# Masks subtracted one slot later, and the Exp of two duos put ahead of the exit, in a top-32 attention followed by a two-layer MLP

## The chip, the cores and the metric

The kernel runs on one core of a Trainium2 chip. Its engines work at the same time, each on its own queue in order: TensorE (PE, matmuls and their weight loads), VectorE (DVE), ScalarE (ACT), GpSimd (POOL) and SyncE (SP, which here only issues DMAs). The metric is the device time of one execution in microseconds (us). The time before is 880.53 us, the median of 3 runs (880.13 to 882.18).

## The reference

Eight batches of eight heads, 576 tokens, head size 64. Each row of scores keeps its 32 largest entries, and the result goes through an MLP whose activation has a learned slope for negative values:

```
scores = (1/8) * q @ k^T                       # 576 x 576 per head
kth    = 32nd largest of each row
scores = where(scores >= kth, scores, -1e9)
attn   = softmax(scores) @ v
x      = heads side by side                    # 4608 x 512
h      = x @ w_in                              # 4608 x 2048
out    = (max(h,0) + alpha * min(h,0)) @ w_out # 4608 x 512
```

All inputs and the output are float32.

## The kernel before

**The unit of work is a duo:** two tiles of 128 query rows, one of each head of a pair of heads ("n"), or the last 64 rows of each head of two pairs ("m", mixed). There are 144 duos (ND), 18 per batch, of which two are mixed. The main loop has one slot per duo, n = 0 to ND + 6, and in slot n each stage works on another duo. Every engine's instructions are kept in the order in which the program writes them, except where the planner moves one ahead of a neighbour that is not ready by its own estimate; the small VectorE instructions of a slot are moved now and then.

**The stages of duo m** (for Exp and norm, m is the even one of two duos m, m+1 that share a tile):

| stage | engine | lines | slot |
|---|---|---|---|
| st_qk: scores to PSUM (one buffer, ps_sc) | PE | 198-218 | m-2 |
| st_exit: scores to SBUF (s_sb) | ACT | 220-225 | m-1 |
| dve_slot: the 8 largest of each of 6 groups (up, small), from these a guess p for the 32nd | DVE | 232-299 | m |
| st_count: sg = sign(p - s), and its sum cs | ACT | 301-308 | m+1 |
| st_y: y = s * sg, so that the entries just below p become y's largest | POOL | 310-315 | m+1 |
| eq, MAX8 p<-y, pk: which of p and the next 8 is the 32nd, by the count | DVE | 271-299 | m+1 |
| kt_sum: KT = 2^60 times the 32nd largest | DVE | 227-230 | m+2 |
| st_relu: r = relu(KT - 2^60 s), zero for kept entries | ACT | 317-322 | m+2 |
| the subtraction s = s - r (masked entries fall far down) | POOL | 323 | m+2 |
| st_exp: w = exp(s/8) of two duos, then two DMA transposes w to wT | ACT, SP | 325-332 | m+4 (even) |
| st_av: xo = wT @ [v, 1] | PE | 334-353 | m+6 |
| norm_a, norm_b: x = xo / row sum, of two duos | DVE | 359-378 | m+7 (odd) |
| st_xT: DMA transpose of x, when a chunk of tokens is complete | SP | 387-409 | m+7 |

**The MLP** works on chunks of 128 or 256 tokens as attention completes them. mlp_ready (415) makes *units* (ph = x @ a piece of w_in, then VectorE's relu gT) and *parts* (a quarter of an output tile pz, four parts a = 0 to 3; the part with a = 3 ends the tile and puts a *store* in a list). The slope's linear share is folded into a matrix w_lin made in the first slots (scale_out, in_trans, lin). h_pe issues a unit, h_dve its relu, o_pe a part (none while a store is open), o_act the copy of a finished tile by ScalarE (o_sb), o_sp its store. `late` (624) asks for a second unit in a slot. keep_warm fills TensorE with idle matmuls ("rest").

**The order within slot n** before (614-660): loads and stores on SP; PE: st_av(n-6), a unit; ACT: st_count(n-1); POOL: st_y(n-1); ACT: st_exit(n+1); PE: perhaps a part; DVE: dve_slot; ACT and POOL: st_relu(n-2) with its subtraction; POOL: cast of v (4 in 18 slots, even ones); PE: transposes for a later pair of heads (prep), st_qk(n+2), then a part or keep_warm; in even slots ACT: st_exp(n-4); ACT: copies of the transposes; in odd slots o_act, and at the end st_xT. After the loop a second loop empties the lists.

Buffers that matter: ps_sc one; s_sb three pairs of duos; sg and r share a tag of three; y three; w two (ws); wT three; ps_h (ph, prep, rest) two.

Of the kernel before, what the change touches and what calls it, by code (L numbers as in the profile page):

```python
# [35 lines left out]
def fast_path(tc, q, k, v, moe_w_in, moe_w_out, moe_alpha, out, flag):  # L36
# [27 lines left out]
    with ExitStack() as ctx:  # L64
# [67 lines left out]
        ws = [const.tile([128, 2, 2, 640], BF16, name=f"w_{i}") for i in range(2)]  # L132
# [99 lines left out]
        def dve_slot(n, f_late):  # L232
# [7 lines left out]
            norm = on(n - 6) and n % 2  # L240
            if on(n):
                s = T["s", n]
                up = two.tile([128, 2, NG // 2, 8], FP32, name="up", tag="up")
                for i in range(2):
                    for g in range(NG):
                        o = 24 * i + 8 * (g // 2)
                        m = DVE.max(out=(lo if g % 2 else up)[:, i, g // 2, :],
                                    in_=s[:, i, GW * g:GW * g + GW])
                        if g % 2:
                            sm(m, [], [(o, o + 8)])  # L250
                        if i == 0 and g == 1:
                            kt_sum(n - 2)
                if norm:
                    norm_a(n - 6)


                bot = two.tile([128, 2, NG // 2, 8], FP32, name="bot", tag="bot")
                sm(DVE.tensor_tensor(bot, up, lo[:, :, :, ::-1], ALU.min), [(0, 48)], [f"bot{n % 2}"])
                sm(DVE.tensor_tensor(th[:, :, 0:24].rearrange("p i (g c) -> p i g c", g=NG // 2), up,
                                     lo[:, :, :, ::-1], ALU.max), [(0, 48)], [(48, 72), (80, 104)])  # L260
                if norm:
                    norm_b(n - 6)
                for i in range(2):
                    o = 48 + 32 * i
                    sm(DVE.max(out=th[:, i, 24:32], in_=bot[:, i, :, :]), [f"bot{n % 2}"], [(o + 24, o + 32)])
            else:
                kt_sum(n - 2)
                if norm:
                    norm_a(n - 6)
                    norm_b(n - 6)  # L270
# [30 lines left out]
        def st_count(n):  # L301
            s, p9 = T["s", n], T["p9", n]
            sg = two.tile([128, 2, S], BF16, name="sg", tag="sg", bufs=3)
# [6 lines left out]
        def st_y(n):  # L310
            y = [three.tile([128, S], FP32, name="y", tag="y") for _ in range(2)]
            sg = T.pop(("sg", n))
            for i in range(2):
                POOL.tensor_tensor(y[i], T["s", n][:, i, :], sg[:, i, :], ALU.mult)
            T["y", n] = y

        def st_relu(n, i):
            s = T["s", n]
            if i == 0:
                T["r", n] = two.tile([128, 2, S], BF16, name="r", tag="sg", bufs=3)  # L320
            r = T["r", n]
            ACT.activation(r[:, i, :], s[:, i, :], AF.Relu, bias=KT[:, 2 * n + i:2 * n + i + 1], scale=-BIG)
            POOL.tensor_tensor(s[:, i, :], s[:, i, :], r[:, i, :], ALU.subtract)

        def st_exp(n):

            w = ws[n // 2 % 2]
# [175 lines left out]
        for b in range(1, B):  # L503
            for i in range(KPB):
# [6 lines left out]
                for u in range(3):  # L511
                    at(s0 + ((1, 3, 3) if b < B - 1 else (0, 1, 2))[u], "prep", lambda p=p, u=u: prep_pe(p, u))
# [101 lines left out]
        for n in range(ND + 7):  # L614
# [5 lines left out]
            if on(n - 6):  # L620
                st_av(n - 6)
            if not h_pe() and not end:
                keep_warm()
            late = len(hq) > (9 if n < 118 else 4) or end

            if on(n - 1):
                st_count(n - 1)
                st_y(n - 1)
            if on(n + 1):
# [11 lines left out]
            if on(n + 2):  # L641
# [6 lines left out]
            if on(n - 3) and n % 2 == 0:  # L648
                st_exp(n - 4)
# [6 lines left out]
            if n % 2 or end:  # L656
                o_act()
            if on(n - 6) and n % 2:
                st_xT(n - 7)
                st_xT(n - 6)  # L660
# [298 lines left out]
```

## Time and profile before

| what | us |
|---|---|
| median of 3 runs | 880.53 |
| the profiled execution's own time | 879.53 |
| its span, first to last instruction | 877.6 |
| y on GpSimd, 288 times 1.281 | 362.6 busy |
| subtraction on GpSimd, 288 times 1.283 | 362.9 busy |
| sg on ScalarE, 288 times 0.771 | 220.7 busy |
| Exp on ScalarE, 72 times 2.116 | 152.4 busy |
| exit on ScalarE, 144 times 1.105 | 159.1 busy |
| gT on VectorE, 144 times 0.676 | 97.3 busy |

The mean granted TensorE clock was 0.977. In the tables of the profile an instruction is named out<-in by the program's tiles; since a helper records every operation, all have line L31, and one goes by the tiles. A wait is written "engine, tile <- who ended it". In the order of time, each line has start, length, engine, operation, and in brackets the idle time before it with what ended it. Consecutive instructions overlap a little at their ends, so what one costs its engine is the distance from start to start: 0.67 and 0.09 for a count, 1.00 for an exit, 0.67 for a relu, 2.02 for an Exp, 0.16 for a MAX8 over 96 entries.

### The profile page before, as it was taken

The numbers are of one execution on the slowest core, as the hardware profiler recorded it, in microseconds if no ns is written. First come the engines' busy times: TensorE is split into PE (matmuls) and PEld (weight loads), VectorE is DVE, ScalarE is ACT, GpSimd is POOL, SyncE is SP. The second block draws the span as 40 slices with busy tenths as digits, with TensorE's granted clock in tenths as the row PEclk, the third lists the DMA queues.
The fourth block names the chain that finished last, engine by engine and source line by source line (L and its number), as shares of the span: only waits on it lengthen the run. The fifth ranks groups of instructions, "written<-read, shape, count | busy, mean of one in ns | idle before, by whom it ended". The sixth has DMA issues, their size and how long they took to land.

```text
span 877.6 us, 18856 instructions
## 1 busy us (share of the span) xinstructions
PE 794.9 (91%) x5531; PEld 448.5 (51%) x5626; DVE 784.2 (89%) x3921; ACT 776.4 (88%) x1239; POOL 752.1 (86%) x672
## 2 busy tenths in 40 slices
PE   8767999989899999899999998899999998999894
PEld 5333455555455555455555555555555554555462
DVE  5989899998999989999999989999999988899941
ACT  6999999898989989999999989999999988788840
POOL 4998998898988989999999989989999988798830
PEclk9989999999999999999999999999999998999997
DMA  7899845544544446446446555447455542434341
GB/s 159 184 205 177 164 107 102 116 111 105 118 112 115 113 84 122 105 110 126 115 103 140 101 113 128 105 112 129 97 118 109 114 114 68 98 80 77 91 91 34
DMA packets 344464, 100.31 MB, mean 114 GB/s; under 512 B 338193, under 2 KB 338209, under 8 KB 344353
## 3 DMA queue, kind: packets, MB, share of 16 engines
q1 hardware_dynamic: 341456, 92.42, 50.0%
q0 software_dynamic: 1696, 6.30, 3.1%
q8 instruction: 46, 0.75, 0.4%
q14 instruction: 66, 0.53, 0.2%
q10 hardware_dynamic: 1200, 0.30, 0.2%
HBM read 36.71 MB, written 9.44 MB: 53 GB/s over the span
## 4 chain that ended last, share of the span: by engine, by line
DVE 35%; PE 29%; POOL 13%; ACT 11%; issue 8%; DMA 3%; SPq 0%; POOLq 0%; ACTq 0%
PE ps_sc L31 10%; DVE p L31 10%; DVE small L31 9%; POOL y L31 8%; PE pz L31 6%; DVE up L31 5%; POOL s_sb L31 5%; DVE gT L31 5%; PE ph L31 4%; PE xo L31 4%; PE rest L31 4%; ACT sg L31 4%; ACT r L31 3%; ACT s_sb L31 2%; DMA wT<-w 1%
## 5 line engine op out<-in xcount | busy, mean ns | idle before, releaser
L31 POOL TENSOR_TENSOR y<-s_sb,sg 128x576 f32<-128x576 f32 x288 | 362.6, 1281 | 88.4 <-ACT sg L31 81.6
L31 POOL TENSOR_TENSOR s_sb<-s_sb,r 128x576 f32<-128x576 f32 x288 | 362.9, 1283 | 1.2 <-ACT r L31 1.0
L31 ACT ACTIVATE sg<-s_sb,p 128x576 bf16<-128x576 f32 x288 | 220.7, 771 | 25.5 <-DVE p L31 20.5
L31 DVE MAX8 p<-y 128x8 f32<-128x576 f32 x288 | 215.6, 748 | 20.2 <-POOL y L31 19.9
L31 DVE MAX8 small<-s_sb 128x8 f32<-128x96 f32 x864 | 216.0, 250 | 0.0
L31 DVE MAX8 up<-s_sb 128x8 f32<-128x96 f32 x864 | 211.7, 245 | 3.1 <-ACT s_sb L31 3.1
L31 ACT ACTIVATE r<-s_sb,KT 128x576 bf16<-128x576 f32 x288 | 208.4, 776 | 0.1
L31 PE MATMUL ps_sc<-qkT 64*128 64x512 f32 (+2 forms) x768 | 185.2, 573 | 21.9 <-ACT s_sb L31 20.6
L31 ACT COPY s_sb<-ps_sc 128x1152 f32<-128x1152 f32 x144 | 159.1, 1105 | 2.3 <-PE ps_sc L31 2.1
L31 PE MATMUL ph<-xT,w_in_b 128*128 128x256 bf16 (+1 forms) x1408 | 152.4, 256 | 2.7 <-DMA xT<-x 2.7
L31 ACT ACTIVATE w<-s_sb 128x2304 bf16<-128x2304 f32 x72 | 152.4, 2116 | 2.0 <-POOL s_sb L31 2.0
L31 PE MATMUL pz<-w_out_b,gT 128*128 128x512 bf16 x556 | 145.0, 381 | 5.8 <-DVE gT L31 2.3
L31 PEld LDWEIGHTS <-wT 128*128 128x128 bf16 (+3 forms) x1600 | 98.7, 100 | 70.6 <-DMA wT<-w 10.8
L31 PE MATMUL xo<-v,wT 128*128 128x65 bf16 (+3 forms) x1600 | 126.8, 198 | 7.3 <-DMA wT<-w 7.2
L31 PE MATMUL rest<-idle 128*128 128x512 bf16 x434 | 121.5, 392 | 3.1 <-ACT qkT L31 1.0
L31 DVE TENSOR_SCALAR gT<-ph 128x512 bf16<-128x512 f32 x144 | 97.3, 676 | 24.8 <-PE ph L31 24.8
L31 PEld LDWEIGHTS <-w_in_b 128*128 128x128 bf16 x1408 | 109.1, 98 | 19.7 <-DMA xT<-x 3.3
L31 PEld LDWEIGHTS ps_sc<-qkT 64*128 64x128 f32 (+1 forms) x768 | 55.4, 170 | 79.9 <-ACT s_sb L31 41.3
L31 PEld LDWEIGHTS ps_sc<-kd,qkT 128*128 128x128 f32 x256 | 39.3, 193 | 101.7 <-issue 93.4
L31 PEld LDWEIGHTS <-gT 128*128 128x128 bf16 x576 | 56.3, 98 | 57.0 <-DVE gT L31 3.6
L31 PE MATMUL ps_sc<-kd,qkT 128*128 128x128 f32 x256 | 64.3, 334 | 1.5 <-DMA kd<-qkT 1.5
L31 PEld LDWEIGHTS <-idle 128*128 128x128 bf16 x468 | 45.7, 101 | 36.0 <-issue 6.0
(56 smaller groups left out, 670.1 us busy)
## 6 DMA issues: line engine op xcount, KB each, us to landing
k_st<-in_k_dram SPq DMA_DIRECT2D x64, 128.0 KB, 2.8
v_st<-in_v_dram SPq DMA_DIRECT2D x64, 128.0 KB, 2.6
out_dram<-o_sb SPq DMA_DIRECT2D x32, 256.0 KB, 2.2
q_st<-in_q_dram SPq DMA_DIRECT2D x62, 128.0 KB, 2.7
w_st<-in_moe_w_out_dram POOLq DMA_DIRECT2D x4, 1024.0 KB, 7.2
wT<-w SPq DMA_TRANSPOSE x144, 3.1
w_in_b<-in_moe_w_in_dram POOLq DMA_DIRECT2D x4, 512.0 KB, 6.4
k_st<-in_k_dram SPq DMA_DIRECT2D x32, 32.0 KB, 2.6
```

Source lines behind the costliest of these rows:

```text
L31: return self.tc.keep_in_program_order(f(*a, **kw))
```

## The change

In each pipeline the later stages move by one slot, and with them the parity of what is done in every second slot. The subtraction leaves st_relu and becomes st_sub(n-3): the first head's stands ahead of y in GpSimd's order, the second's behind it. st_exp runs in odd slots, for duos n-5 and n-4, right behind st_count and ahead of st_exit. st_av, norm and st_xT are one slot later, norm in even slots and, in VectorE's order, behind the min/max pair (norm_a) and behind the two MAX8 of bot (norm_b). o_act and the transposes for later pairs move to even slots, `late` to odd ones; in odd slots st_qk(n+2) stands behind the part or filler. sg and r have four buffers, w one. The loop has one slot more.

```diff
-        ws = [const.tile([128, 2, 2, 640], BF16, name=f"w_{i}") for i in range(2)]
+        ws = [const.tile([128, 2, 2, 640], BF16, name=f"w_{i}") for i in range(1)]
...
-            norm = on(n - 6) and n % 2
+            norm = on(n - 7) and n % 2 == 0
...
-                if norm:
-                    norm_a(n - 6)
 
 
                 bot = two.tile([128, 2, NG // 2, 8], FP32, name="bot", tag="bot")
...
                 if norm:
-                    norm_b(n - 6)
+                    norm_a(n - 7)
                 for i in range(2):
                     o = 48 + 32 * i
                     sm(DVE.max(out=th[:, i, 24:32], in_=bot[:, i, :, :]), [f"bot{n % 2}"], [(o + 24, o + 32)])
+                if norm:
+                    norm_b(n - 7)
             else:
                 kt_sum(n - 2)
                 if norm:
-                    norm_a(n - 6)
-                    norm_b(n - 6)
+                    norm_a(n - 7)
+                    norm_b(n - 7)
...
-            sg = two.tile([128, 2, S], BF16, name="sg", tag="sg", bufs=3)
+            sg = two.tile([128, 2, S], BF16, name="sg", tag="sg", bufs=4)
...
         def st_y(n):
             y = [three.tile([128, S], FP32, name="y", tag="y") for _ in range(2)]
             sg = T.pop(("sg", n))
+            if on(n - 2):
+                st_sub(n - 2, 0)
             for i in range(2):
                 POOL.tensor_tensor(y[i], T["s", n][:, i, :], sg[:, i, :], ALU.mult)
             T["y", n] = y
+            if on(n - 2):
+                st_sub(n - 2, 1)
 
         def st_relu(n, i):
             s = T["s", n]
             if i == 0:
-                T["r", n] = two.tile([128, 2, S], BF16, name="r", tag="sg", bufs=3)
+                T["r", n] = two.tile([128, 2, S], BF16, name="r", tag="sg", bufs=4)
             r = T["r", n]
             ACT.activation(r[:, i, :], s[:, i, :], AF.Relu, bias=KT[:, 2 * n + i:2 * n + i + 1], scale=-BIG)
+
+        def st_sub(n, i):
+            s, r = T["s", n], T["r", n]
             POOL.tensor_tensor(s[:, i, :], s[:, i, :], r[:, i, :], ALU.subtract)
 
         def st_exp(n):
 
-            w = ws[n // 2 % 2]
+            w = ws[0]
...
-                    at(s0 + ((1, 3, 3) if b < B - 1 else (0, 1, 2))[u], "prep", lambda p=p, u=u: prep_pe(p, u))
+                    at(s0 + ((0, 2, 2) if b < B - 1 else (0, 1, 2))[u], "prep", lambda p=p, u=u: prep_pe(p, u))
...
-        for n in range(ND + 7):
+        for n in range(ND + 8):
...
-            if on(n - 6):
-                st_av(n - 6)
+            if on(n - 7):
+                st_av(n - 7)
             if not h_pe() and not end:
                 keep_warm()
-            late = len(hq) > (9 if n < 118 else 4) or end
+            late = len(hq) > (9 if n < 118 else 4) and n % 2 == 1 or end
 
             if on(n - 1):
                 st_count(n - 1)
                 st_y(n - 1)
+            elif on(n - 3):
+                st_sub(n - 3, 0)
+                st_sub(n - 3, 1)
+            if on(n - 4) and n % 2:
+                st_exp(n - 5)
             if on(n + 1):
                 st_exit(n + 1)
...
-            if on(n + 2):
+            if on(n + 2) and n % 2 == 0:
                 st_qk(n + 2)
             if (n, "lin") in todo:
                 run(n, "lin")
             elif not (end or ready() > 2) or not o_pe():
                 if not end:
                     keep_warm()
-            if on(n - 3) and n % 2 == 0:
-                st_exp(n - 4)
+            if on(n + 2) and n % 2:
+                st_qk(n + 2)
...
-            if n % 2 or end:
+            if n % 2 == 0 or end:
                 o_act()
-            if on(n - 6) and n % 2:
+            if on(n - 7) and n % 2 == 0:
+                st_xT(n - 8)
                 st_xT(n - 7)
-                st_xT(n - 6)
```

## The prediction

> **What bounds the kernel now.** I first read the busy shares, then who waited for whom, then the order of time within two slots in the steady middle, and last the same for the places where a slot is unusually long. The busy shares come first:
>
> ```profile
> PE 794.9 (91%) x5531; PEld 448.5 (51%) x5626; DVE 784.2 (89%) x3921; ACT 776.4 (88%) x1239; POOL 752.1 (86%) x672
> ```
>
> No engine stands out. Four engines are within 5% of each other, so a slot (one duo, about 5.6 us) is set by small waits handed from one engine to the next. The view of waits shows which are large:
>
> ```profile
> POOL y L31 <- ACT sg L31: 81.6, 76, 11.2
> ACT o_sb L31 <- PE pz L31: 48.5, 13, 13.6
> DVE gT L31 <- PE ph L31: 24.8, 16, 4.1
> ACT sg L31 <- DVE p L31: 20.5, 29, 1.8
> DVE p L31 <- POOL y L31: 19.9, 33, 2.3
> DVE rz L31 <- PE xo L31: 16.4, 18, 3.9
> DVE small L31 <- ACT sg L31: 10.1, 20, 1.4
> ```
>
> The columns are total us, times, longest. GpSimd's 81.6 us in front of the sign products y looks like the prize, but GpSimd is not what the others wait for: VectorE waits for y only 19.9 us in all. In the stretch from 150 to 750 us VectorE waits 35 us in total (14.2 for y, 7.9 for ph, 7.3 for the counts, 5.8 for xo), so 6% of it is all that a perfect reordering could return there. The order of time shows how the 81.6 us arise (start, length, engine, operation):
>
> ```profile
> 425.52 2.11 ACT L31 ACTIVATE w<-s_sb 128x2304 bf16<-128x2304 f32 x1
> 427.53 0.76 ACT L31 ACTIVATE sg<-s_sb,p 128x576 bf16<-128x576 f32 x1
> 428.46 2.52 POOL L31 TENSOR_TENSOR y<-s_sb,sg 128x576 f32<-128x576 f32 x2 [0.88 <-ACT sg L31]
> 433.45 2.52 POOL L31 TENSOR_TENSOR y<-s_sb,sg 128x576 f32<-128x576 f32 x2
> ```
>
> ScalarE's slot with an Exp (even) lasts two counts 1.52, exit 1.00, two relus 1.34 and Exp 2.02, together 5.88 us from one sg to the next, while VectorE's slot without a norm lasts 5.14 (pk to pk). So the counts after an Exp start about 0.75 us late; y shows it as 0.88. VectorE hides most of that, because it needs y only some 2.9 us into its slot. The third kind of place is one slot in which ScalarE stands at a store:
>
> ```profile
> 511.61 0.59 ACT L31 COPY o_sb<-pz 128x512 f32<-128x512 f32 x1 [2.82 <-PE pz L31]
> 513.03 2.51 POOL L31 TENSOR_TENSOR y<-s_sb,sg 128x576 f32<-128x576 f32 x2 [2.91 <-ACT sg L31]
> 514.35 0.76 DVE L31 MAX8 p<-y 128x8 f32<-128x576 f32 x1 [2.33 <-POOL y L31]
> ```
>
> Here the last quarter of an output tile was issued behind st_qk at the end of an odd slot, and the o_act of that slot waits for it with the next counts queued behind. VectorE loses 2.33 us. And in the head the transposed weights come late:
>
> ```profile
> 63.85 0.79 PE L31 MATMUL xo<-v,wT 128*128 128x65 bf16 x10 [2.33 <-DMA wT<-w]
> 64.68 0.18 DVE L31 RECIPROCAL rz<-xo 128x4 f32<-128x4 f32 x1 [2.78 <-PE xo L31]
> ```
>
> **The change part by part**, in us of the whole run against the profiled execution's 879.53 (span 877.6 and 1.9 around it; the median of the runs, 880.53, is 1.0 higher, and I give the result on that scale).
>
> *The subtraction one slot later.* Before, GpSimd's ring is y, y, sub, sub; after, sub, y, y, sub. Between the last y of one duo and the first of the next stand two subtractions (1.28 each) in both. y still starts when sg is there, so the 81.6 us stay: 0. What it frees is relu: it may now come 2.02 later. Relu is waited for 1.0 us in all, so nothing is gained from that alone.
>
> *Exp ahead of the exit in odd slots.* ScalarE's sum per two slots is unchanged, and the long gap between counts stays 5.88; it moves from even to odd slots, and so do norm, copies and stores from odd to even, so the pairing of long ScalarE slot and following norm slot is as before: 0 for that. New is that the exit in the odd slot ends at 1.52 + 2.02 + 1.10 = 4.65 after the counts start, where VectorE begins the next duo at 5.14. The cover is 0.4. Counts late by more than 0.4 eat it; then VectorE waits up to about 0.25. That holds in the slots behind a late store (17) and in a few with all copies; bounds 0 and 72 pairs x 0.1 = 7; taken: +4. Queued behind that exit is st_qk on TensorE, put behind the filler for it: qk (1.4, mixed 2.1) then ends about 0.1 to 0.9 after the next counts start, and its exit is due 1.5 after them: hidden, and if that cover went, the exit would be late by the difference.
>
> *The prices of the parity.* The cast of v (0.84 and a gap, 0.93, 4 in 18 slots) stays in even slots. There it lay in the slot with Exp, where y was late anyway: the gap from y to y is 5.88 with a cast and 5.88 with an Exp. After, the two fall into different slots: y is up to 0.5 late for VectorE's p in 28 slots, of which most comes back as an earlier count in the next. Bounds 0 and 28 x 0.25 = 7; taken +3, below the middle because the return is visible in the 4.95 that follows such slots.
>
> *The stores.* Counting the lists of units, parts and stores slot by slot, the bad coincidence (last part at the slot's end, o_act right behind) falls in slots 25, 33, 41, 51, 87, 123, 125, 129, 139, 141 before, and VectorE's waits behind them are 1.5, 2.6, 0.6, 2.6, 2.6, 1.8, 1.5, 1.0 and twice 0.3: 14.8. After, it falls in seventeen even slots: 26, 34, 42, 50, 52, 62, 70, 78, 86, 88, 98, 106, 114, 124, 134, 138, 140. Their size depends on what TensorE has ahead of it. Like slot 33 (two transposes behind gT, a mixed qk) are 50 and 86: 2.5 each. With a second part and a transpose (52, 88, 124), 1.6, like slot 25. With transposes and a mixed xo (42, 78) 1.5. With one transpose (34, 70, 106, 114) 0.5, as slot 41 was. The other six 0.15. Sum 5.0 + 4.8 + 3.0 + 2.0 + 0.9 = 15.7: +0.9. Bounds: every one as small as slot 139 (17 x 0.3 = 5, -10), and the first eleven as large as slot 33 (11 x 2.6 + 1 = 30, +15).
>
> *One more slot between Exp and xo.* The transposes get 5.5 - 3.0 = 2.5 us more. That removes the 2.78 in the head; against it stands the head's Exp slot, which now also has two weight scalings (7.1 against 5.0 to 5.2 for its neighbour, instead of 6.5 against 5.6), about 0.25 x 5. Together -1.5 (bounds -2.8 and +2). At the end it removes xo's wait of 2.49, counted below.
>
> *norm behind the min/max pair.* rz waits 5.8 us in the middle. It comes 0.24 later in VectorE's order, while xo is later by at most 0.9 behind a mixed qk. Most goes: -3 (bounds -5.8 and 0). What is late next in these slots is ph for gT, unchanged in kind.
>
> *late only in odd slots.* Ten extra units instead of twelve, two fewer of them inside the 144 slots: two gT at 0.59 from start to start, -1.
>
> *The longer drain.* From slot 144 to the last xo TensorE has 5 xo, 8 units and 9 parts before, and that is what sets 832.0 to 854: 5 x 0.78 + 8 x 0.97 + 9 x 1.1 = 21.6. After: 6 xo, 10 units, 10 parts = 25.4. That is +3.8, less the 2.49 that xo no longer waits: +1.3 (bounds 0 and 5). The last mask subtraction comes one GpSimd operation later (+1.3), hidden beneath TensorE's backlog; without that backlog it would count.
>
> *Buffers.* One w instead of two: the next Exp must wait until both transposes have read it. Exps are two slots, 11.1, apart; a transpose is issued about 1 after the Exp and lands in a median of 3.1, so some 6 remain: 0. In the head, where landing takes up to 11.6, an Exp could wait 2 to 3 once or twice; taken 0, bound +5. SP's queue keeps its order of loads, stores, transposes; loads of the following slot stand behind a transpose that waits for its Exp, 2 us earlier in its slot than before. sg gets a fourth buffer because r now lives a slot longer: 0.
>
> The Trainium skill speaks against the single w: "Trainium Kernel Development and Optimization", Best Practices, advises two buffers so that a transfer runs beside compute. By that rule each Exp would stand behind its predecessor's transposes. The rows above put the price at nothing away from the head, and no run here shows it yet.
>
> Sum: 4 + 3 + 0.9 - 1.5 - 3 - 1 + 1.3 = +3.7, to 884.
>
> **The rivals.**
>
> *A. The waits go (faster).* The counts' comparison eq is waited for 10.1 us. In about half the norm slots the planner pulls it ahead of the norm and the pair of min and max (at 2.1 us of the slot), where it stalls 0.33 to 0.6 on the late counts; where it stands in written order, at 3.0, it doesn't stall. With the norm later in the order it may stay there. Then 7 for eq, 5.8 for rz and 2.8 in the head go, the exit costs nothing, and casts (3) and drain (1.3) stay: 880.5 - 15.6 + 4.3 = about 869. For it: VectorE's two slots add up to only 10.6 without waits, against 11.1 now. Against it: eq is pulled ahead in all even slots as well, without a norm. It decides if eq in norm slots is no longer waited for and the seventeen stores cost no more than the ten.
>
> *B. The stores (slower).* The seventeen cost 1.5 on average: 25 - 14.8 = +10, with the rest +2.8: 893. For it: slot 33's 2.33 without any second part. Against it: slot 41's 0.6.
>
> *C. No difference.* The gains of slack (head, rz, drain) cancel the parity's prices: 880.5. The change is mainly a shift of everything by one slot, which speaks for it.
>
> *D. A new hold.* Exp stands at w, or exit for VectorE in each pair by 0.3 (72 x 0.3 = 22): above 900.
>
> **How the numbers follow.** My case, 883 to 889, 0.30; B, 889 to 900, 0.17; C, within 0.3% (about 2.6 us, what a measurement here can tell from no change), 0.20; A 0.29; D 0.04. That is faster 0.29, same 0.20, slower 0.51. The range must hold 8 in 10: from 866 (two thirds of A) to 899 (nearly all of B); some 0.15 is left out.
>
> **What would show it.** GpSimd's wait for sg still near 80. The wait of ACT o_sb for PE pz in more and smaller pieces in even slots, about 16 us behind them on VectorE. VectorE's first maximum (up) waiting for s_sb, absent before except once at the start, for some 4 us in pieces under 0.3. rz's wait down from 16.4 by half. Exp without a wait for a transpose. Wrong it would be if eq's wait vanished (then A), if up's wait stood in each pair (D), or if the planner placed parts differently from the written order, which would change which slots hold stores.

## The result, and the profile after

The changed kernel takes 902.31 us (median of 4 runs, 899.91 to 906.33) against 880.61 for the kernel before beside it: a ratio of 1.0248, 95% interval 1.0209 to 1.0287. That is 21.7 us slower, outside my range of 866 to 899. The sign was right, the size was not: I had +3.7. The profiled execution has a span of 898.1 us (time 899.91), 20.5 more than before.

The busy shares of the changed kernel are nearly those of before, and every engine has merely more time to stand:

```profile
PE 804.6 (90%) x5638; PEld 451.2 (50%) x5638; DVE 788.5 (88%) x3921; ACT 785.2 (87%) x1239; POOL 753.2 (84%) x671
```

The view of waits of the changed kernel (total us, times, longest):

```profile
ACT o_sb L31 <- PE pz L31: 61.5, 21, 11.4
PE ps_sc L31 <- ACT s_sb L31: 51.5, 44, 2.6
POOL y L31 <- ACT sg L31: 47.7, 33, 11.5
POOL s_sb L31 <- ACT r L31: 43.3, 57, 2.7
DVE p L31 <- POOL y L31: 31.5, 58, 2.3
DVE rz L31 <- PE xo L31: 27.6, 21, 5.7
ACT s_sb L31 <- PE ps_sc L31: 12.7, 7, 4.7
PE plin L31 <- DMA wT<-w: 7.0, 2, 4.0
```

Four things differ from the view of before. GpSimd's 81.6 us ahead of the sign products have split in two: 47.7 under the old name, and 43.3 in front of the subtraction, which now comes first in its slot. VectorE's wait for y grew from 19.9 to 31.5. TensorE's wait for the exit to free ps_sc grew from 20.6 to 51.5. And the last two lines have grown from next to nothing: an exit now waits up to 4.7 us for its scores (12.7 in all, 2.1 before), and plin waits on TensorE (0.3 before; a third wait of 3.0 stands under the name of w_lin_b).

Such totals don't say when the time goes. For that I took the start of the first sign product of each duo from the order of time on GpSimd, and cut the run into four stretches (us; the columns after the first are differences between duos). y of duo n stands in slot n + 1. What follows, and most expectations, call it y of slot n; only the expectation of e1 counts by the slot in which it stands, where the changed kernel has 158.4.

| kernel | y of duo 24 starts at | 24 to 122 | 122 to 143 | 143 to the end |
|---|---|---|---|---|
| before | 153.5 | 554.5 | 126.8 | 42.9 |
| changed | 164.2 | 563.1 | 121.6 | 49.2 |
| difference | +10.7 | +8.7 | -5.2 | +6.3 |

So half of the loss is made before duo 24, where I had forecast a small gain, and up to duo 17 there is none (113.46 against 113.94). The last two stretches together make only 1.1.

**The head.** The order of time on TensorE and ScalarE in the changed kernel (start, length, engine, operation, wait) in slots 19 and 20:

```profile
120.77 2.11 ACT L31 ACTIVATE w<-s_sb 128x2304 bf16<-128x2304 f32 x1
122.91 1.12 ACT L31 COPY s_sb<-ps_sc 128x1152 f32<-128x1152 f32 x1
123.92 1.44 ACT L31 ACTIVATE r<-s_sb,KT 128x576 bf16<-128x576 f32 x2
125.26 0.57 ACT L31 CAST w_lin_b<-plin 128x512 bf16<-128x512 f32 x1
```
```profile
121.93 1.05 PE L31 MATMUL ph<-xT,w_in_b 128*128 128x256 bf16 x8
125.89 3.57 PE L31 MATMUL plin<-w_la,w_inT 128*128 128x512 bf16 x8 [2.91 <-DMA wT<-w]
129.39 2.08 PE L31 MATMUL ps_sc<-qkT 64*128 64x512 f32 x4
```
```profile
132.02 1.12 ACT L31 COPY s_sb<-ps_sc 128x1152 f32<-128x1152 f32 x1 [4.67 <-PE ps_sc L31]
```

Slots 17, 19, 21 and 23 hold the copy that frees the only ps_z bank (lin_out), and slots 17, 19 and 21 also the next products that write into it (lin). The copy used to stand behind counts, exit and relus; now Exp stands there as well, 2.1 us. The plin products start at 125.89, just as the copy ends at 125.83. The profile puts their wait down to a transpose, but this is the release that fits in time; e16 below tests it. TensorE's queue holds still meanwhile: eight products then take 3.57 us instead of 1.89, because the clock fell. The score products behind them, at the end of the odd slot, are late in turn, and the exit waits 4.67 us for them.

The granted clock stands in the view by stretches (the column before the last two), for 124 to 130 us and 142 to 148 us, in which the waits of 2.91 and 4.05 us end:

```profile
124.00:130.00 6.00, 4.11 (x10) 1.49 (x11) 2.89 (x20) 3.35 (x8) 4.60 (x4) 0.57 0.70 158
142.00:148.00 6.00, 5.56 (x27) 2.36 (x27) 1.55 (x12) 2.67 (x6) 4.34 (x4) 0.72 0.46 104
```

The Trainium skill, "TensorE: Matmul & The Clock Gate", section "HAM oscillation — how this bites in real kernels", warns of gaps on TensorE of more than about 3.4 us. Here the clock fell around waits of 2.9 and 4.1 us, while the products behind the wait of 3.04 us at 112.67 ran at full speed (1.89 us, clock 1.00 from 112 to 118 us). So one drop came after a gap shorter than the page's figure: the region is right, the limit is not sharp.

**The middle.** The late last parts came in the slots that I had counted. This is slot 86, on ScalarE, GpSimd and VectorE:

```profile
521.65 0.58 ACT L31 COPY o_sb<-pz 128x512 f32<-128x512 f32 x1 [3.02 <-PE pz L31]
523.08 2.52 POOL L31 TENSOR_TENSOR y<-s_sb,sg 128x576 f32<-128x576 f32 x2 [3.33 <-ACT sg L31]
524.39 0.76 DVE L31 MAX8 p<-y 128x8 f32<-128x576 f32 x1 [2.33 <-POOL y L31]
```

VectorE's waits from slot 24 to slot 122, first in the kernel before, then in the changed one:

```profile
DVE p L31 <- POOL y L31: 10.8, 13, 2.3
DVE small L31 <- ACT sg L31: 7.3, 15, 0.8
DVE gT L31 <- PE ph L31: 5.5, 5, 1.3
DVE rz L31 <- PE xo L31: 3.7, 8, 1.2
```
```profile
DVE p L31 <- POOL y L31: 23.1, 38, 2.3
DVE rz L31 <- PE xo L31: 5.7, 11, 1.0
DVE gT L31 <- PE ph L31: 2.1, 5, 0.5
DVE up L31 <- ACT s_sb L31: 1.6, 10, 0.2
DVE small L31 <- ACT sg L31: 0.2, 1, 0.2
```

The wait of the counts' comparison eq (small) is gone, as rival A has it, and the wait for y has doubled, as rival B has it. The sums are 27.3 and 32.7, so 5.4 of the stretch's 8.7 us show here. VectorE is also busy 1.8 us longer (526.0 against 524.2), and the remaining 1.5 lie in gaps too small for the view to list. up waits 1.6 us in all.

### The profile page after: what moved, and what is told of

It is laid out like the page before. It is cut to its first block, busy times and chain, and to the rows that moved or that the text cites. A ratio compares the mean times of both kernels' runs of the same rounds, so it can differ in the third digit from the quotient of the medians.

```text
span 898.1 us, 18721 instructions
## 1 busy us (share of the span) xinstructions
PE 804.6 (90%) x5638; PEld 451.2 (50%) x5638; DVE 788.5 (88%) x3921; ACT 785.2 (87%) x1239; POOL 753.2 (84%) x671
## 4 chain that ended last, share of the span: by engine, by line
DVE 32%; PE 32%; ACT 23%; POOL 7%; issue 3%; DMA 2%; ACTq 0%; SPq 0%; POOLq 0%
PE ps_sc L31 11%; DVE p L31 9%; DVE small L31 9%; ACT w L31 8%; ACT sg L31 6%; PE pz L31 6%; DVE up L31 6%; ACT s_sb L31 5%; POOL y L31 5%; PE ph L31 5%; PE xo L31 4%; DVE gT L31 4%; PE rest L31 3%; ACT r L31 2%; POOL s_sb L31 2%
## 5 line engine op out<-in xcount | busy, mean ns | idle before, releaser
L31 POOL TENSOR_TENSOR y<-s_sb,sg 128x576 f32<-128x576 f32 x288 | 362.2, 1278 | 60.8 <-ACT sg L31 47.7
L31 POOL TENSOR_TENSOR s_sb<-s_sb,r 128x576 f32<-128x576 f32 x288 | 365.7, 1277 | 43.5 <-ACT r L31 43.3
L31 DVE MAX8 p<-y 128x8 f32<-128x576 f32 x288 | 216.0, 750 | 31.8 <-POOL y L31 31.5
L31 PE MATMUL ps_sc<-qkT 64*128 64x512 f32 (+2 forms) x768 | 183.4, 569 | 52.9 <-ACT s_sb L31 51.5
L31 ACT COPY s_sb<-ps_sc 128x1152 f32<-128x1152 f32 x144 | 159.8, 1110 | 14.9 <-PE ps_sc L31 12.7
L31 PE MATMUL pz<-w_out_b,gT 128*128 128x512 bf16 x576 | 148.8, 381 | 2.3 <-DVE gT L31 2.3
L31 PE MATMUL rest<-idle 128*128 128x512 bf16 x480 | 126.4, 390 | 0.9 <-ACT qkT L31 0.8
L31 ACT COPY o_sb<-pz 128x512 f32<-128x512 f32 x36 | 21.0, 583 | 61.5 <-PE pz L31 61.5
L31 PEld LDWEIGHTS <-idle 128*128 128x128 bf16 x480 | 46.2, 100 | 45.4 <-issue 5.7
```

The source lines that it names most:

```text
L31: return self.tc.keep_in_program_order(f(*a, **kw))
```

## The experiments

Theory T: the loss has separate places, the head, the late last parts in the middle, and the drain. Its main rival: each of the 72 pairs pays a little, because the exit writes into the buffer that Exp has just read and starts 0.13 us later for it. All edits are to the changed kernel unless it is said otherwise. Where the text says by how much a run is shorter or longer, and names no other, it compares its median with the 902.31 above. The kernel before took 878.2 to 879.0 beside these runs and 880.6 beside the changed kernel, so such a difference is some 2 us too favourable to the run; the ratios are free of this. The stretches are those of the one profiled execution, which lies up to 3.6 us from the median (e6 893.59, e12 899.68).

| run | edit | us | ratio to before (95%) | y of duo 24 | 24 to 122 | 122 to 143 | to the end |
|---|---|---|---|---|---|---|---|
| changed | | 902.31 | 1.0248 (1.0209 to 1.0287) | 164.2 | 563.1 | 121.6 | 49.2 |
| e1_head | copy twice, scores first to slot 23 | 909.56 | 1.0382 (1.0327 to 1.0436) | 170.0 | 566.1 | 123.1 | 48.4 |
| e2_casts | casts in odd slots | 905.58 | 1.0284 (1.0231 to 1.0337) | 173.7 | 561.8 | 121.5 | 49.3 |
| e3_parts | filler first in even slots | 890.13 | 1.0124 (1.0082 to 1.0165) | 167.2 | 554.7 | 119.9 | 48.0 |
| e4_sub_old | subtraction at its old place | 949.57 | 1.0808 (1.0771 to 1.0844) | 171.9 | 599.3 | 125.7 | 50.8 |
| e5_lin_ahead | copy twice | 914.92 | 1.0414 (1.0366 to 1.0462) | 174.6 | 565.9 | 123.1 | 48.0 |
| e6_lin_shift | plin and copy a slot later | 890.15 | 1.0120 (1.0073 to 1.0166) | 151.3 | 567.3 | 123.1 | 50.1 |
| e7_b_parts | before, filler first in odd slots | 873.75 | 0.9948 (0.9914 to 0.9983) | 151.8 | 558.5 | 119.8 | 43.5 |
| e8_drain | end a slot shorter | 908.21 | 1.0338 (1.0291 to 1.0385) | 165.7 | 564.4 | 121.6 | 52.0 |
| e9_both | e3 and e6 | 878.01 | 0.9990 (0.9973 to 1.0006) | 151.6 | 556.2 | 119.9 | 48.6 |
| e10_b_norm | e7 and norm behind the pair | 866.93 | 0.9851 (0.9828 to 0.9874) | 154.1 | 552.0 | 119.3 | 42.9 |
| e11_qk_first | scores first in odd slots | 937.30 | 1.0688 (1.0639 to 1.0738) | 159.2 | 600.9 | 127.4 | 47.7 |
| e12_norm_old | norm at its old place | 903.24 | 1.0281 (1.0253 to 1.0309) | 163.5 | 565.2 | 121.8 | 47.3 |
| e13_late_any | e9, extra units in any slot | 875.80 | 0.9970 (0.9954 to 0.9987) | 152.4 | 555.3 | 119.7 | 46.2 |
| e14_b_norm_alone | before, norm behind the pair | 883.69 | 1.0050 (1.0028 to 1.0072) | 157.9 | 557.9 | 125.0 | 42.0 |
| e15_both_norm_old | e9, norm at its old place | 893.62 | 1.0159 (1.0128 to 1.0191) | 153.9 | 569.4 | 120.2 | 50.3 |
| e16_lin_ahead_once | copy ahead of Exp | 890.67 | 1.0135 (1.0117 to 1.0154) | 153.0 | 563.8 | 121.6 | 50.3 |
| e17_head_once | e16, scores first to slot 23 | 902.19 | 1.0289 (1.0251 to 1.0328) | 164.6 | 564.8 | 121.6 | 49.1 |

### The late last parts

e3_parts changes the order on TensorE in even slots alone:

```
-            if on(n + 2) and n % 2 == 0:
+            if on(n + 2) and n % 2 == 0 and n < 24:
                 st_qk(n + 2)
             ...
-            if on(n + 2) and n % 2:
+            if on(n + 2) and (n % 2 or n >= 24):
                 st_qk(n + 2)
```

> The changed kernel with the filler (an output part or idle products) ahead of the score products in even slots too, from slot 24 on, so that the last part of an output tile is finished 1.4 to 2.1 us earlier, before the output copy that follows it on ScalarE. Theory T: the wait of ScalarE's o_sb for pz, 26.9 us between 150 and 750, falls below 8, VectorE's waits for y behind stores (about 14 us in the middle) go for the most part, and the time falls by 8 to 12, to 890 to 894. Rival S (the stores' waits are covered, or the exit then waits for late scores instead): ScalarE's waits for ps_sc appear in the odd slots in pieces, and the time stays within 3 of 902 or grows.

It took 890.13 us, 12.2 less. The stretch from slot 24 to 122 is 554.7 us, which is that of the kernel before (554.5). The order of time on ScalarE and TensorE in e3 shows slot 86 again: the last part's products now stand ahead of the mixed score products, and o_act waits 0.62 us instead of 3.02.

```profile
517.12 0.59 ACT L31 COPY o_sb<-pz 128x512 f32<-128x512 f32 x1 [0.62 <-PE pz L31]
```
```profile
516.05 1.03 PE L31 MATMUL pz<-w_out_b,gT 128*128 128x512 bf16 x4
517.01 2.17 PE L31 MATMUL ps_sc<-qkT 64*64 64x512 f32 x16
```

VectorE's waits in e3 from slot 24 to 122, to be read against the 23.1 us for y above:

```profile
DVE rz L31 <- PE xo L31: 9.2, 11, 1.2
DVE gT L31 <- PE ph L31: 7.5, 12, 1.9
DVE p L31 <- POOL y L31: 5.5, 18, 0.5
DVE up L31 <- ACT s_sb L31: 0.2, 1, 0.2
```

What replaces the wait for y is in part a wait for xo and ph. The order on TensorE in even slots, of last part or filler, score products and output copy, thus makes the middle's whole excess over the kernel before. How much of that is the stores' alone is not shown, since e3 turns the order in every even slot, and the pieces of 0.5 us behind the casts go too. The pairs' bubble is not needed for it: Exp and exit are adjacent in e3 too.

### The head

The first two tries at the head were meant to move the copy of w_lin_b ahead of Exp. In both the edit left the copy at its old place as well, so it was made eight times instead of four, and the bank came free no earlier:

```
+            if n < 24:
+                run(n, "lin_out")
             if on(n - 4) and n % 2:
                 st_exp(n - 5)
             ...
             run(n, "lin_out")
```

> The changed kernel with two steps of slots up to 23 put back: the copies of w_lin_b stand ahead of Exp again, and the score products stand ahead of the plin products in odd slots. Theory T (the loss has three places: the head, about 8 to 11 us, the late stores and the casts in the middle, about 12, and the drain, about 6): the start of y of slot 24 returns from 158.4 towards 148 to 151, TensorE's waits for w_lin_b and ScalarE's waits of 1.9, 4.7 and 3.3 for ps_sc near 116, 132 and 147 us go, and the time falls by 7 to 10, to 892 to 895. Rival R (the loss is spread evenly, because the exit written into the buffer that Exp has just read starts 0.13 us later in each of 72 pairs, and the lost time in the head would be given back later): y of slot 24 may come earlier, but the time stays within 3 of 902.

> The changed kernel with one step of the head put back: the copies of w_lin_b stand ahead of Exp, while the score products stay behind the plin products in odd slots. Theory H (the head's loss is that the next plin, in the same odd slot, waits for this copy, which stands behind Exp, exit and both relus; TensorE stands 3 to 4 us, its clock falls to about a half, and score products and exit come late): the waits of 3.0, 2.9 and 4.1 us go, the y of slot 24 comes at 155 to 158 instead of 164.2, and the time falls by 6 to 9 to about 895. Rival G (what made the head of the first experiment even longer was the copy in front of Exp, not the order of score products and plin): y of slot 24 stays at 164 or later, and the time at 902 or above.

They took 909.56 and 914.92 us. They don't decide between theory H and rival G, though the longer waits ahead of plin (4.1 and 4.5 us in e5) fit H. The two runs that do decide: e6 moves plin and copies by one slot, so that both fall against Exp as before, and e16 moves the copy alone, once.

```
-                at(15 + 2 * kk + a, "lin", lambda kk=kk, a=a: lin(kk, a))
-            at(17 + 2 * kk, "lin_out", lambda kk=kk: lin_out(kk))
+                at(16 + 2 * kk + a, "lin", lambda kk=kk, a=a: lin(kk, a))
+            at(18 + 2 * kk, "lin_out", lambda kk=kk: lin_out(kk))
```

> The changed kernel with the plin products and the copies of w_lin_b one slot later, so that both fall in the same parity against Exp as before. Theory H: y of slot 24 returns to 154 to 157, TensorE's clock stays at 1.00 in the head, and the time falls by 8 to 10, to 892 to 894. Rival (the order of score products in odd slots makes the head slow by itself): y of slot 24 above 160, time above 898.

```
+            run(n, "lin_out")
             if on(n - 4) and n % 2:
                 st_exp(n - 5)
             ...
             run(n, "cast")
-            run(n, "lin_out")
```

> The changed kernel with the copies of w_lin_b moved ahead of Exp, each made once. (In the two earlier runs that were to do this, e1 and e5, the copy stood in front of Exp and was made a second time at its old place, eight copies instead of four, so that the bank that plin waits for came free no earlier.) Theory H (plin waits for the copy behind Exp, exit and relus): TensorE's waits of 3 to 4.5 us ahead of plin go, y of slot 24 comes at 153 to 158 instead of 164.2, the time falls by 6 to 11, to 891 to 896. Rival G (the order alone doesn't matter): y of slot 24 at 163 or later, 901 or above.

e6 took 890.15 us and e16 890.67, both 12 less (10 to 11 by the ratios). y of slot 24 starts at 151.3 and 153.0, against 153.5 in the kernel before. TensorE in e16 at the products that waited 2.91 us above, and its clock around them:

```profile
120.37 1.89 PE L31 MATMUL plin<-w_la,w_inT 128*128 128x512 bf16 x8
```
```profile
118.00:124.00 6.00, 5.45 (x36) 2.73 (x35) 5.79 (x31) 5.97 (x10) 5.13 (x5) 1.00 0.29 66
```

plin no longer waits anywhere, it takes 1.89 us, and the clock is 1.00. The head's loss is the place of this copy, and theory H holds.

> As the run beside it, and the score products ahead of plin in odd slots up to slot 23 (what e1 meant to do). The changed kernel with score products first in all odd slots had y of slot 24 at 159.2, 5 earlier than with plin first. If the late exits in the head come from the score products standing behind plin, this adds to the copy's move: y of slot 24 at 150 to 154, time 889 to 893. If plin now waits behind score products that wait for the exit behind Exp, it is later than the run beside it by 2 or more.

e17 adds this to the edit of e16:

```
-            if on(n + 2) and n % 2 == 0:
+            if on(n + 2) and (n % 2 == 0 or n < 24):
                 st_qk(n + 2)
             ...
-            if on(n + 2) and n % 2:
+            if on(n + 2) and n % 2 and n >= 24:
                 st_qk(n + 2)
```

With the score products ahead of plin as well, y of slot 24 is back at 164.6 and the time at 902.19. They wait for the exit, which is behind Exp, and plin stands behind them; at 143.68 plin takes 3.62 us, at a clock that fell to 0.55 (142 to 148 us):

```profile
141.08 2.08 PE L31 MATMUL ps_sc<-qkT 64*128 64x512 f32 x4 [2.72 <-ACT s_sb L31]
143.68 3.62 PE L31 MATMUL plin<-w_la,w_inT 128*128 128x512 bf16 x8
```

In e11 below, where the score products stand first too but the copy keeps its place behind Exp, y of slot 24 is at 159.2. Why it comes 5.4 later once the copy is moved as well stays open.

### Both repairs together

> The changed kernel with both repairs that worked alone: plin and its copies one slot later, and the filler ahead of the score products in even slots too. Theory T (head and late last parts are two separate losses, 12 each): 902.3 - 12.1 - 12.2 = 878, no further than 2.5 from it, that is, what the kernel before has; y of slot 24 at 151 to 153, and 554 to 556 us from there to slot 122. Rival (the two overlap, or a loss in each pair lies beneath them): 884 or above.

878.01 us, ratio 0.9990 (0.9973 to 1.0006): the two losses add up to what was expected of them within a microsecond, and the change with both repaired is level with the kernel before. Against before it keeps +1.7 us in the middle and +5.6 in the drain, and gains 1.9 in the head and 6.9 between slots 122 and 143.

### The moves that I had costed at nothing

e4 puts the subtraction back behind the sign products of its slot. Its edit is the change's own, reversed:

```
         def st_y(n):
             ...
-            if on(n - 2):
-                st_sub(n - 2, 0)
             for i in range(2):
                 POOL.tensor_tensor(y[i], T["s", n][:, i, :], sg[:, i, :], ALU.mult)
             T["y", n] = y
-            if on(n - 2):
-                st_sub(n - 2, 1)
...
-            elif on(n - 3):
-                st_sub(n - 3, 0)
-                st_sub(n - 3, 1)
...
                 st_relu(n - 2, 1)
+                st_sub(n - 2, 0)
+                st_sub(n - 2, 1)
```

> The changed kernel with the mask subtractions at their old place, behind the sign products of the same slot; all else is as changed. Theory T: the later subtraction costs and brings nothing, because the sign products start when sg is there in both orders: 902 within 2.5, and GpSimd's 43 us of waiting for r turn into waiting for sg again (about 80). Rival P (the subtraction ahead of the sign products holds them while it waits for a late relu): the time falls by 4 or more.

949.57 us, 47 more. The order of time on GpSimd in e4 shows why: in the slot with Exp the relus come 2.1 us later, GpSimd stands in front of the subtraction (for r 123.3 us in the whole run, 43.3 in the changed kernel), and the next sign products queue behind it. VectorE's wait for y rises from 31.5 to 71.7.

```profile
410.20 2.52 POOL L31 TENSOR_TENSOR s_sb<-s_sb,r 128x576 f32<-128x576 f32 x2 [1.92 <-ACT r L31]
412.68 2.51 POOL L31 TENSOR_TENSOR y<-s_sb,sg 128x576 f32<-128x576 f32 x2
```

e11 puts the score products ahead of the filler in odd slots again (the order of e17, but for the whole run and with the copy at its place).

> The changed kernel with the score products ahead of the filler in odd slots in the whole run, as before. My prediction costed their move behind the filler at 0. Theory T: 0 from slot 24 to 122 (563 within 2), and a head that is 2 to 5 longer, since plin then stands behind score products that wait for the exit behind Exp: 902 to 907. Rival Q (the move delays the exits of even slots, where they follow the counts directly): the time falls by 4 or more.

937.30 us, 35 more. The middle, where I expected nothing, is 37.8 longer and the stretch behind it 5.8; the head came 5 us earlier, where I expected a loss. TensorE's and VectorE's longest waits in e11 between 170 and 705 us:

```profile
PE ps_sc L31 <- ACT s_sb L31: 54.1, 38, 2.7
DVE rz L31 <- PE xo L31: 37.4, 35, 3.3
```

In the changed kernel these lines read 30.8 in 29 and 5.7 in 11 there. With the score products in front, the filler that could run meanwhile stands behind them, and the next xo, for which VectorE waits, comes behind both. Without either of these two moves the changed order is far slower still; what they would do with Exp at its old place has no run.

### Casts

```
-                at(s0 + 8, "cast", lambda p=p: cast_v(p))
+                at(s0 + 9, "cast", lambda p=p: cast_v(p))
...
-            at(2 * p + 2, "cast", lambda p=p: cast_v(p))
+            at(2 * p + 3, "cast", lambda p=p: cast_v(p))
```

> The changed kernel with the casts of v one slot later, in the slots that have the Exp, as it was before. Theory T: VectorE's pieces of 0.45 to 0.5 us of waiting for y in some 25 slots with a cast go, and the time falls by 6 to 11 of 902, to 891 to 896. My prediction's price for this was 3: then 899. Rival R (the bubble of 0.13 between Exp and exit): the short slots have slack to give the 0.5 back, so 902 within 1.5.

905.58 us. In the middle it won 1.3 us, not the 6 to 11 of theory T; VectorE's pieces of 0.5 us behind casts went, and its wait for y fell from 23.1 to 18.3, but other waits grew, so that the sum fell only from 32.7 to 30.1. The head lost 9.5, by another way. The loads of v on SyncE's queue wait for the stage that the cast frees (12.8 us between 30 and 100 us, 6.0 in the changed kernel), transposes stand behind them, and one Exp waited for the only w. This account is read from the trace; no run tests it. The view of waits of e2 for SyncE's queue and the order of time on ScalarE:

```profile
SPq L31 <- POOL v L31: 12.8, 3, 7.7
```
```profile
55.30 2.12 ACT L31 ACTIVATE w<-s_sb 128x2304 bf16<-128x2304 f32 x1 [6.03 <-DMA wT<-w]
```

### The drain

e8 issues the last Exp one slot earlier, and xo, norm and the transposes of the last two duos too:

```
-        for n in range(ND + 8):
+        for n in range(ND + 7):
...
+            if n == ND + 5:
+                st_av(n - 6)
...
-            if on(n - 4) and n % 2:
+            if on(n - 4) and n % 2 and n < ND + 3:
                 st_exp(n - 5)
+            if n == ND + 2:
+                st_exp(n - 4)
```

> The changed kernel with the end one slot shorter: the last Exp one slot earlier, and xo, norm and transposes of the last two duos one slot earlier, so that the unit and the parts of one slot run behind the last xo instead of ahead of it. Theory D (the end lost 6.3 us because TensorE has 28.8 us of work in front of the last xo instead of 22.0): from the y of slot 143 to the end 49.2 becomes 43 to 45, the time falls by 4 to 6. Rival (that work has to be done anyway and only moves behind the last xo, where TensorE has no room): no change, 902 within 1.5.

908.21 us. The stretch to the end got longer (52.0), and so theory D fell: the units and parts have to be done anyway. The rival, which forecast no change, doesn't explain the longer stretch either. TensorE's busy time from the sign products of slot 143 to the end, in the kernel before and in the changed one, in the view by stretches (the number behind the comma):

```profile
834.67:877.60 42.93, 29.86 (x288) 19.37 (x291) 12.38 (x26) 9.57 (x12) 7.52 (x7) 0.89 0.28 64
```
```profile
848.86:898.10 49.24, 35.25 (x333) 22.55 (x333) 13.94 (x28) 10.15 (x13) 8.72 (x8) 0.91 0.27 68
```

5.4 us more work is left there, nearly all of the 6.3. Counted by weight loads, since the trace of before lacks some records of products, it is three more parts (15 products into pz), one more unit (16 into ph) and one more xo (10). Part of it is the extra units in odd slots alone, which e13 allows in even slots again:

```
-            late = len(hq) > (9 if n < 118 else 4) and n % 2 == 1 or end
+            late = len(hq) > (9 if n < 118 else 4) or end
```

> The kernel with both repairs (878.0), and the extra units of the first product allowed in even slots too, as before. It has 119.9 us from the y of slot 122 to that of slot 143 and 48.6 from there to the end; the kernel before has 126.8 and 42.9. Theory W (the same TensorE work lies in the one or in the other): the first stretch grows by 2 to 5, the second falls by as much, the time stays within 1.5 of 878. Rival D (the drain has a loss of its own, a late Exp and a slow clock): the second stretch stays at 48 to 49 and the time changes only by the first. My prediction gave this edit 1 us (879).

875.80 us, 2.2 less than e9: the drain is 2.4 shorter, TensorE's busy time in it 31.08 us instead of 32.94, and the stretch ahead of it is no longer (119.7). Neither theory had it so; the extra units cost nothing where they now lie. The rest of the drain's excess has no run of its own.

### norm

> The changed kernel with norm at its old place in VectorE's order, ahead of the min and max pair. My prediction gave the later place 3 us (rz waits less): then 905. By the profile of the changed kernel, where rz waits as long as before in the middle (6.0 against 5.8), it gave nothing: 902 within 1.5. Rival: norm's later place holds the counts' comparison less: eq's wait of 7 us returns and the time rises by 5 or more.

In the changed kernel norm's old place (the change's three lines reversed) gives 903.24 us (1.0281, against 1.0248 with overlapping intervals): no effect that stands clear of the noise.

> The kernel before with norm behind the min and max pair in VectorE's order, and nothing else. My prediction's price for this was 3, of rz's 5.8 us: 876. Where the late last parts set the pace (theory M, masking), it gives nothing: 878.8 within 1.3. If it gives as much as on top of the repaired parts: 872.

> The kernel before with the filler ahead of the score products in odd slots (873.75 by itself) and with norm behind the min and max pair in VectorE's order, as in the changed kernel. If VectorE's 15.1 us of waiting for xo between 170 and 705 are what sets its pace there, they fall to 8 or less and the time is 868 to 871. Rival (norm's place only moves the wait, to gT, y or the counts): 873.75 within 2.

> The kernel with both repairs (878.0) and norm at its old place, ahead of the pair. Theory M (norm's later place is worth something only once the late last parts are gone): 882 to 885. If norm's place is worth nothing in this order of ScalarE: 878 within 1.3.

In the kernel before, norm behind the pair makes 883.69 (1.0050, 1.0028 to 1.0072): slightly slower, which no theory had. With the last parts repaired the same edit is worth 6.8 there (873.75 to 866.93), and in e9 undoing it costs 15.6, where theory M had 4 to 7. VectorE's waits between 170 and 705 us in e9, and in e15 with norm at its old place:

```profile
DVE rz L31 <- PE xo L31: 9.2, 11, 1.2
DVE gT L31 <- PE ph L31: 8.0, 13, 1.9
DVE p L31 <- POOL y L31: 4.9, 17, 0.4
DVE up L31 <- ACT s_sb L31: 0.3, 2, 0.2
```
```profile
DVE rz L31 <- PE xo L31: 13.6, 19, 1.8
DVE gT L31 <- PE ph L31: 12.6, 19, 1.8
DVE small L31 <- ACT sg L31: 8.6, 17, 1.6
DVE p L31 <- POOL y L31: 1.5, 5, 0.4
```

eq's wait (small) is back with 8.6 us, and xo and ph are waited for 4.4 and 4.6 longer, y and up 3.7 shorter: 13.9 us more in sum, near the 15.6. In the changed kernel theory M holds: between 170 and 705 us VectorE waits 32.2 us in e12 and 32.0 in the changed kernel, and what eq and xo take more in e12, y takes less. For the kernel before it doesn't: that the edit alone costs 5 us there stays open. In its profile ScalarE's copies into qkT wait 12.5 us for TensorE from slot 24 to 122, instead of 6.0.

### The kernel before, with its last parts early

> The kernel before with the filler ahead of the score products in odd slots from slot 24 on, so that its last parts are ready before its output copies. Theory T (the late last parts cost VectorE 14.8 us there): the wait of o_sb for pz falls from 17.7 us between 150 and 750 to below 5, and the time falls by 6 to 10, to 868 to 872. Rival S (the exit follows the counts directly in the next slot of this kernel, so later scores hold it): ScalarE waits for ps_sc in pieces in the even slots, and the time stays at 878 or grows.

```
-            if on(n + 2):
+            if on(n + 2) and (n % 2 == 0 or n < 24):
                 st_qk(n + 2)
             ...
+            if on(n + 2) and n % 2 and n >= 24:
+                st_qk(n + 2)
             if on(n - 3) and n % 2 == 0:
                 st_exp(n - 4)
```

873.75 us, 0.9948 (0.9914 to 0.9983), a gain below theory T's 6 to 10. It lies between slots 122 and 143 (119.8 against 126.8); the middle is 4 longer, since VectorE there now waits 15.1 us for xo and ScalarE 12.2 for ps_sc, so rival S holds in part. Norm behind the pair takes 6.2 of that wait for xo away, and e10 at 866.93 us is 1.5% faster than the kernel before and the fastest here.

e10 is also the like for e9: both have the last parts early and norm behind the pair. e9 is 1.4% slower (0.9990 against 0.9851): 5.7 us in the drain and 4.2 in the middle, less 2.5 in the head. So the rest of the change costs something even with both repairs. In the middle it shows on VectorE as the wait for ph (8.0 us in e9, 1.9 in e10, between 170 and 705 us), while up waits 0.3; a small loss in each pair is not excluded by this.

## Why the prediction was wrong

Two terms of the sum make nearly all of the miss: the head, taken as -1.5 and measured as +10.7, and the middle, where the stores were taken as +0.9 and the stretch grew by 8.7, nearly all of which went with the order of e3.

**The head: wrong, and the largest step.** "Together -1.5 (bounds -2.8 and +2)" was +10.7. I looked there only at xo's wait and at the weight scalings. Among the prices of the parity I listed the casts and left out lin_out, the copy that stays in odd slots and now stands behind Exp. A move of Exp past everything that ScalarE issues in that slot had to be costed for each of them. e16 puts the price of this one at 11.6 by the medians and about 10 by the ratios.

**The stores: the count right, the price of it wrong.** The waits behind them in VectorE came nearly as forecast, slot by slot: .92, .48, 1.46, 2.33, 1.58, .54, .48, 1.46, 2.33, 1.58, .53, .47, .40 and 1.56 in the fourteen slots from 26 to 124 (26, 62 and 98 were forecast at 0.15), 16.1 in sum, where I had 15.7 for all seventeen. But the term "+0.9" set this against 14.8 of which a third lay behind slot 122. Read in the same way, the middle alone went from 8.8 to 14.6 behind its stores. All its waiting for y went from 10.8 to 23.1, and the new order in e3 gave 8.4 there and 12.2 in all by the medians (11 by the ratios).

**The exit behind Exp: mechanism right, size off.** up waits 1.6 us in ten pieces of at most 0.2, where I took 4. Its second half, the score products behind the filler, I called hidden, at no cost or gain: undone it costs 35.

**The subtraction: the zero was worked out in the wrong order.** "Relu is waited for 1.0 us in all, so nothing is gained from that alone" is read from the old order of ScalarE. In the new one the relus of every second slot are 2.1 later, and without the move the kernel loses 47 more (e4).

**Casts: right in kind, too large.** Taken +3, measured 1.3 in the middle. The visible pieces in VectorE tempted me afterwards into 6 to 11, and e2 refuted that.

**norm: wrong.** Taken -3. rz's wait between slots 24 and 122 rose from 3.7 to 5.7, and e12 shows no effect. It gains only where the late last parts are gone.

**late only in odd slots: wrong sign.** Taken -1; undone in e9 it is worth 2.2.

**The drain: near in sum, wrong in its parts.** Taken +1.3. From y of slot 143 it is +6.3, while the stretch ahead, in whose end the kernel before has xo's wait of 2.49 (at 832.0), got 5.2 shorter: +1.1 for both, near my figure, but not from the parts that I added up. The +3.8 of work was 5.4, counted to the end: three parts and one unit more, where I had one part and two units. The waiting did not go away: xo waits 1.36 at 849.38, ph 1.41 behind it, and the clock is 0.72 between 853 and 857.

**One w: right in the changed kernel**, where no Exp waits for a transpose, so the rule of the Trainium skill, "Trainium Kernel Development and Optimization", Best Practices, to double-buffer so that DMA overlaps compute, didn't bite. The cover that I named is thin all the same. With SyncE's queue held in e2 an Exp waited 6.03 us, my bound of +5.

**The rivals.** Of A, eq's wait went as said (7.3 to 0.2), but A's other condition, "the seventeen stores cost no more than the ten", failed: putting the last parts early gave 11 to 12 us here and about 5 in the kernel before. D's time, above 900, was met, but not by its cause: up does not wait in each pair, and no Exp stands at w. B named the right place in the middle, but not its size: 25 us behind the stores was forecast, and 16.1 were measured up to slot 124. That 902 less the head comes near B's 893 is luck in part. C did not hold.

## What to carry to other kernels

When a long instruction is moved ahead in an in-order queue, list every instruction of that slot that now stands behind it, in each stage of the run, and follow the buffer that each one frees: one small copy that guards a single PSUM bank cost 10 to 12 us here. Cost the parts of a reordering against the new order, not the old: two moves that I had priced at nothing by the old order were worth 35 and 47 us in the new one. And when a copy waits for a product at the end of a queue, try the order of the two groups ahead of it first: that edit paid in both kernels.

## What the runs showed of the hardware

- TensorE's clock fell after waits of 2.9 and 4.1 us (eight products 3.57 and 3.29 us instead of 1.89), but not after one of 3.04. The late products then delayed their reader by 4.67 us, more than the wait itself.
- An exit that writes the buffer which an Exp has just read starts about 2.14 us after that Exp's start (120.77 to 122.91; it is at most 2.16 in all 69 pairs); counts that follow an Exp and write elsewhere start 2.01 after it (425.52 to 427.53, in the kernel before), and so do copies of the transposes there. A loss from these pairs was not found, but it is not excluded: e9 has them all and is level with the kernel before, yet 1.4% behind e10.
- The profile named a transpose for two waits of plin that ended with the copy of w_lin_b. The move of that copy alone took them away.
